# Four-layer linear-attention and MLP kernel: three chunks scaled in the second pass of layer 1, and the first MLP chunk's rows turned by VectorE and DMA

## The chip, the cores and the metric

The kernel runs on one core of a Trainium2 chip, in one launch. The metric is the device time of an execution in microseconds; times of several runs are given as their median. In the profile PE is TensorE's matrix product, PEld its weight load, DVE is VectorE, ACT is ScalarE, POOL is GpSimd and SP is SyncE, which issues all DMA transfers of this kernel.

## The reference

Four residual layers, A B A B, on x of 2048 tokens by 576 columns, with weights shared between the two A and the two B layers. A is linear attention with 32 heads of 18 columns; B normalizes once more and is an MLP with 4608 hidden columns.

```python
def _A_ref(x, wqkv, wo):
    B, S, D = x.shape
    H = 32; Dh = D // H
    qkv = (lambda x, *d: x.transpose(*d))((x @ wqkv).reshape(B, S, 3, H, Dh), 2, 0, 3, 1, 4)
    q, k, v = qkv[0], qkv[1], qkv[2]
    phi = lambda t: jnp.where(t > 0, t + 1, jnp.exp(t)) + 1e-6
    pq, pk = phi(q), phi(k)
    kv = jnp.einsum("bhsd,bhse->bhde", pk, v)
    z = jnp.einsum("bhsd->bhd", pk)
    num = jnp.einsum("bhqd,bhde->bhqe", pq, kv)
    den = jnp.einsum("bhqd,bhd->bhq", pq, z)[..., None] + 1e-6
    o = num / den
    return (lambda x, *d: x.transpose(*d))(o, 0, 2, 1, 3).reshape(B, S, D) @ wo

def _B_ref(x, w1, b1, w2, b2):
    y = _layernorm(x, axis=-1)
    h = _gelu(jnp.einsum("bsd,df->bsf", y, w1) + b1)
    return jnp.einsum("bsf,fd->bsd", h, w2) + b2

x = A_x
x = x + _A_ref(_layernorm(x, axis=-1), A_wqkv, A_wo)
x = x + _B_ref(_layernorm(x, axis=-1), B_w1, B_b1, B_w2, B_b2)
x = x + _A_ref(_layernorm(x, axis=-1), A_wqkv, A_wo)
x = x + _B_ref(_layernorm(x, axis=-1), B_w1, B_b1, B_w2, B_b2)
```

All inputs are bfloat16; the residual rows are kept in float32 in DRAM between the layers.

## The kernel before

The tokens are worked in 16 tiles of 128 rows and in 4 chunks of 512 (four tiles, `TPC`). The text calls the four layers 1 to 4; in the code `li` is 0 to 3. Normalized rows are needed with columns on partitions, as `yT` (5 blocks of 128 columns, the fifth only half filled with data). There are two ways to get them there, and the argument `evac` of `lnp.feed` chooses:

- `"act"` or `"dve"`: five TensorE transposes into PSUM (L493) and a copy to `yT`, by ScalarE at L498;
- `"dma"`: `turn_rows` lets VectorE transpose 32 by 32 blocks of a tile into the tile `turned` (L295); after the fourth tile of a chunk four DMAs store it to DRAM (`y_d`, L303), and `land` loads it back into `yT` (L320, L323) some ticks later. Tokens then stand in another order within the chunk, and `spread` and `gather` put that right where ScalarE reads PSUM.

`LNPipe` takes each tile through statistics, reciprocal deviation, the factors, the norm and the turn, one stage a `tick`. With statistics on VectorE these are L392, L393, L399 and L413; on ScalarE L374 and L383 with L385 on GpSimd. Then GpSimd does `ln_rstd` (L428), `ln_nmr` (L431), the norm of an MLP row (L461) and the copy of its last 64 columns to the upper half of the fifth block, the tail copy (L469). `hold` delays the first stage by so many ticks, `tp_at` sets after which output tile the TensorE transpose may stand.

Layer 1 (`layer_A` with `li == 0`) has a first pass over the keys of half the columns with most query products, and a second pass, `sums(n)`, which multiplies the other half of the keys with the rows. Into this second pass are woven: `den_stage(c)`, the denominators of a query chunk (20 small products, then Ln and Exp on ScalarE give `rden`); `quad_stage(c)`, which lays `rden` out for a product; `quarter_stage(c)`, 16 small products that broadcast `rden` into four PSUM banks, and four ScalarE copies (L792) of them into `turned`, which is free then; `scale_stage(4, c)`, the same for the last head group (L776); `quarter_scale(c, ...)`, which multiplies the queries with it on VectorE (L798); and `kv_groups` and `kv_wo_half` (L713, copied at L719), which fold the key-value matrix into the output weights. Before the change, chunks 0 and 1 go through these steps in the second pass, and 2 and 3 among the output tiles.

The output stage, `wo_stage(t)` for 16 tiles, has ten products a tile (L924) into one of two PSUM pairs by turns, `accA` and `accB`. VectorE adds the residual row (`residual`, L598), which frees the pair for the tile after next, and SP stores the new row. The first four tiles' rows feed the next MLP's first chunk, through `lnp.feed(..., "act", ...)`, that is TensorE transposes. Residual rows come in pairs of tiles (`prefetch_xo`), four tiles ahead.

PSUM has four banks by turns under the tag `h` (queries, denominators, broadcasts, folds, transposes and half of the MLP's first products) and the pairs `accA` and `accB`. The order of TensorE's instructions is the order of the code, held by `pe_chain`; on the other engines a scheduler places the instructions, within added orderings such as these:

```python
            if dve_last["sum"] is not None:
                tc.add_manual_dep(turn.ins, dve_last["sum"], NOSYNC, reason="rows are turned behind the sums")
```

The MLP (`LayerB`) takes one chunk after the other: nine groups of `m1_group` (L1053, gelu at L1049), then four tiles of 72 products (L1111). While a chunk is worked on, the next chunk's rows are loaded, normalized and turned through `"dma"`.

Of the kernel before, what the change touches and what calls it, by code (L numbers as in the profile page):

```python
# [8 lines left out]
ALU = mybir.AluOpType  # L9
# [25 lines left out]
def build(tc, A_x, A_wqkv, A_wo, B_w1, B_b1, B_w2, B_b2, out, dbg=None, n_layers=4):  # L35
    nc = tc.nc
    dbg = dbg or {}
    with ExitStack() as ctx:
# [90 lines left out]
        yT = const.tile([P, KD, S], BF16, name="yT")  # L129
# [162 lines left out]
        def turn_rows(y, t, kind):  # L292

            c, j = divmod(t, TPC)
            turn = nc.vector.transpose(out=turned[:, :, j, :], in_=y[:, 0:D])  # L295
# [15 lines left out]
        def land(now=False):  # L311

            for it in list(landing):
                it[0] -= 1
                if it[0] > 0 and not now:
# [3 lines left out]
                cols = slice(c * CB, (c + 1) * CB)  # L319
# [22 lines left out]
        class LNPipe:  # L342
# [11 lines left out]
            def tick(self, transposes=1):  # L354
                land()
                for it in list(self.items):
# [94 lines left out]
                    elif st in (2, 3):  # L451
# [16 lines left out]
                        if it["kind"] == "B" and it["evac"] != "dma":  # L468
                            nc.gpsimd.tensor_copy(out=y[:, D:DPAD], in_=y[:, 4 * P:D])  # L469
# [6 lines left out]
                    elif st == 4:  # L476
# [17 lines left out]
                        if first:  # L494
                            named(f"ca{t}", nc.scalar.copy(out=yT[:, 0:3, t * P:(t + 1) * P], in_=tp[:, 0:3, :]))  # L495
                            named(f"cd{t}", nc.vector.tensor_copy(out=yT[:, 3:KD, t * P:(t + 1) * P], in_=tp2[:, 3:KD, :]))
                        elif it["evac"] == "act":
                            turned_tile = nc.scalar.copy(out=yT[:, :, t * P:(t + 1) * P], in_=tp)  # L498
# [5 lines left out]
                        else:  # L504
                            nc.vector.tensor_copy(out=yT[:, :, t * P:(t + 1) * P], in_=tp)
# [102 lines left out]
        def layer_A(li, next_kind, pre_a1=None):  # L608
            pq = {}

            def q_proj(g, c, defer=False):
                qp = ps_h.tile([P, 512], F32, name="q_ps", tag="h")
                for k in range(KD):
                    pe(nc.tensor.matmul(qp[0:GR[g], :], lhsT=wqkv_sb[:, k, GO[g]:GO[g] + GR[g]],  # L614
                                     rhs=yT[:, k, c * CA:(c + 1) * CA],
# [26 lines left out]
            def k_half(t, half, defer=False):  # L642
                kp = ps_h.tile([P, 512], F32, name="k_ps", tag="h")
                for k in range(KD):
                    pe(nc.tensor.matmul(kp[:, 0:HALF], lhsT=yT[:, k, t * P:(t + 1) * P],  # L645
# [91 lines left out]
            def den_stage(c, after=None, pair=None):  # L737
# [10 lines left out]
                rden = work.tile([P, P], BF16, name="rden", bufs=1)  # L748
# [3 lines left out]
                act_last["rden"] = nc.scalar.activation(out=rden[:], in_=dp[:, P:2 * P], func=ACT.Exp,  # L752
# [4 lines left out]
            def quad_stage(c, after=None):  # L757
# [3 lines left out]
                    in1=rden_of.pop(c)[:].unsqueeze(1).to_broadcast([P, 4, P]), op=ALU.mult)  # L761
# [19 lines left out]
            def quarter_stage(c):  # L781
# [8 lines left out]
                spread_rows = turned[:].rearrange("p a t c -> p (a t c)").rearrange("p (i w) -> p i w", i=4)  # L790
# [3 lines left out]
            def quarter_scale(c, groups, after):  # L794
                spread_rows = turned[:].rearrange("p a t c -> p (a t c)").rearrange("p (i w) -> p i w", i=4)
# [54 lines left out]
            if li == 0:  # L850
# [369 lines left out]
```

## Time and profile before

| | |
|---|---|
| runs | 764.25, 763.88, 764.13 us; median 764.13 |
| profiled execution | 763.8 us, its span 762.1 us |
| granted TensorE clock | 1.0 |
| first product of the first MLP (h_ps) | 104.3 us after the span's start |
| layer 1, second pass; output stage | 59 to 81 us; 81 to 104 us |
| DMA | 80897 packets, 73.82 MB, 36730 of them under 512 B |

Times within the profile are microseconds from the span's start. Busy time of TensorE is a modelled end of each pipelined product, so the step from the start of one product to the start of the next is what a product costs: 0.123 for 288 columns, 0.216 for 512. A wait for several things is put down to the one that came last.

### The profile page before, as it was taken

The page shows a single profiled execution, that of the slowest core. Times are in us where ns is not written, and L with a number is a line of the kernel's source. Part 1 is how long each engine was busy: PE and PEld are TensorE (multiplying, and loading weights), DVE is VectorE, ACT ScalarE, POOL GpSimd, SP SyncE. Part 2 cuts the span into 40 slices and gives each one's busy share as a digit, 9 for nine tenths or more (in the row PEclk, how much of TensorE's full clock was granted, in tenths as well). Part 3 has the DMA queues.
Part 4 walks back from the last instruction along what each step waited for, and adds up shares of the span by engine and source line. Part 5 has one row for each costly group of instructions (what it writes and reads, how often), then busy time and mean ns, then how long its engine had stood idle before and what let it go on. Part 6 is the DMA issues. An engine that isn't in the chain of part 4 may idle for free.

```text
span 762.1 us, 15720 instructions
## 1 busy us (share of the span) xinstructions
PE 755.5 (99%) x6551; PEld 489.2 (64%) x6551; DVE 271.3 (36%) x684; ACT 328.7 (43%) x734; POOL 117.7 (15%) x194
## 2 busy tenths in 40 slices
PE   9999999999999999999999999999999999999998
PEld 5776764675477457646777767447645754674476
DVE  8875763136023503401355678600230132000000
ACT  6886657204600650264056567560164037205600
POOL 4840141002000301200110005300020021001000
PEclk9999999999999999999999999999999999999999
DMA  8993483017302711330246008430240033011000
GB/s 252 259 317 53 157 280 83 16 48 198 90 24 76 198 54 45 100 79 11 69 128 205 1 29 277 163 83 16 75 115 18 16 125 83 9 32 56 1 10 23
DMA packets 80897, 73.82 MB, mean 97 GB/s; under 512 B 36730, under 2 KB 65466, under 8 KB 80826
## 3 DMA queue, kind: packets, MB, share of 16 engines
q1 hardware_dynamic: 80826, 72.82, 32.3%
q8 instruction: 51, 0.84, 0.4%
q14 instruction: 20, 0.16, 0.1%
HBM read 48.03 MB, written 24.77 MB: 96 GB/s over the span
## 4 chain that ended last, share of the span: by engine, by line
PE 97%; DVE 1%; ACT 1%; DMA 0%; issue 0%
PE m_ps L1111 36%; PE h_ps L1053 20%; PE hp_ps L1053 16%; PE q_ps L614 6%; PE wo_ps L924 5%; PE k_ps L645 5%; PE k_ps L670 4%; PE m_half L1111 1%; PE k_tail L670 1%; PE tp L493 1%; PE kv_ps L695 0%; PE den_ps L745 0%; PE rden_ps L772 0%; PE rden_ps L788 0%; DMA x<-in_A_x_dram 0%; PE kvwo_half L713 0%
## 5 line engine op out<-in xcount | busy, mean ns | idle before, releaser
L1111 PE MATMUL m_ps<-w_sb,hT 128*128 128x288 bf16 x2232 | 274.8, 286 | 0.0
L1111 PEld LDWEIGHTS <-hT 128*128 128x128 bf16 x2304 | 224.8, 98 | 59.8 <-issue 3.4
L1053 PEld LDWEIGHTS <-w_sb 64*128 64x128 bf16 x2304 | 124.7, 94 | 136.4 <-issue 1.9
L1053 PE MATMUL hp_ps<-yT,w_sb 64*128 64x512 bf16 x1152 | 178.0, 376 | 0.0
L1053 PE MATMUL h_ps<-yT,w_sb 64*128 64x512 bf16 x1152 | 147.9, 376 | 0.0
L1058 ACT COPY relay_sb<-relay_sb 128x1 f32<-128x1 f32 x144 | 28.5, 198 | 259.9 <-PE h_ps L1053 217.6
L1049 ACT ACTIVATE hT<-h_ps,b1T 128x512 bf16<-128x512 f32 x144 | 91.0, 683 | 44.4 <-PE h_ps L1053 44.4
L428 POOL TENSOR_TENSOR ln_rstd<-ln_u,neg_half 128x1 f32<-128x1 f32 x61 | 35.3, 580 | 413.4 <-DVE ln_u L410 225.1
L1049 ACT ACTIVATE hT<-hp_ps,b1T 128x512 bf16<-128x512 f32 x144 | 91.1, 692 | 0.0
L598 DVE TENSOR_TENSOR xbf<-m_ps,xo 128x576 bf16<-128x576 f32 x15 | 11.4, 758 | 214.4 <-PE m_ps L1111 214.4
L598 DVE TENSOR_TENSOR xo<-m_ps,xo 128x576 f32<-128x576 f32 x16 | 12.1, 758 | 175.7 <-PE m_ps L1111 175.7
L581 POOL TENSOR_TENSOR xo<-xo,b_bc 128x576 f32<-128x576 f32 x32 | 40.9, 1282 | 98.8 <-DMA xo<-x_d 60.5
L1053 PE MATMUL h_ps<-yT,w_tail 64*128 64x512 bf16 x144 | 54.1, 376 | 0.0
L1053 PE MATMUL hp_ps<-yT,w_tail 64*128 64x512 bf16 x144 | 54.1, 376 | 0.0
L614 PE MATMUL q_ps<-yT,wqkv_sb 128*126 128x512 bf16 (+1 forms) x200 | 49.4, 379 | 0.0
L645 PE MATMUL k_ps<-wqkv_sb,yT 128*128 128x288 bf16 x320 | 47.1, 286 | 0.3 <-ACT yT L495 0.3
L924 PE MATMUL wo_ps<-kvwo,pq 126*128 126x288 bf16 (+1 forms) x320 | 43.7, 286 | 0.0
L1053 PEld LDWEIGHTS <-w_tail 64*128 64x128 bf16 x288 | 27.1, 94 | 17.0
L645 PEld LDWEIGHTS <-yT 128*128 128x128 bf16 x320 | 30.9, 98 | 8.9 <-ACT yT L495 1.1
L924 PEld LDWEIGHTS <-pq 126*128 126x128 bf16 (+1 forms) x320 | 30.0, 97 | 9.3 <-DVE pq L798 0.2
L614 PEld LDWEIGHTS <-wqkv_sb 128*126 128x126 bf16 (+1 forms) x200 | 25.6, 131 | 11.9 <-issue 0.3
L547 ACT ACTIVATE phi_e<-q_ps 126x512 bf16<-126x512 f32 (+1 forms) x40 | 23.9, 598 | 15.4 <-PE q_ps L614 15.4
(141 smaller groups left out, 597.9 us busy)
## 6 DMA issues: line engine op xcount, KB each, us to landing
xo<-x_d SPq DMA_DIRECT2D x48, 288.0 KB
x_d<-xo SPq DMA_DIRECT2D x32, 288.0 KB
xl<-x_d SPq DMA_DIRECT2D x24, 288.0 KB
y_d<-turned SPq DMA_DIRECT2D x40, 144.0 KB
w_sb<-in_B_w_dram SPq DMA_DIRECT2D x6, 864.0 KB
yT<-y_d SPq DMA_DIRECT2D x10, 512.0 KB
w_sb<-in_B_w_dram SPq DMA_DIRECT2D x9, 512.0 KB
x_d<-xn SPq DMA_DIRECT2D x16, 288.0 KB
```

Of the source, the lines that this page charges most:

```text
L428: nc.gpsimd.tensor_tensor(out=rstd[:], in0=it["u"][:], in1=neg_half[:], op=ALU.pow)
L547: exp = nc.scalar.activation(out=e_out, in_=ps_ap, func=ACT.Exp)
L581: nc.gpsimd.tensor_tensor(out=xo[:], in0=xo[:], in1=b2_bc[:], op=ALU.add)
L598: total = nc.vector.tensor_tensor(out=xn[:, cols].rearrange("p (h n) -> p h n", h=2), in0=halves, in1=xo[:, cols].rearrange("p (h n) -> p ...
L614: pe(nc.tensor.matmul(qp[0:GR[g], :], lhsT=wqkv_sb[:, k, GO[g]:GO[g] + GR[g]], rhs=yT[:, k, c * CA:(c + 1) * CA], start=(k == 0), stop=(k ...
L645: pe(nc.tensor.matmul(kp[:, 0:HALF], lhsT=yT[:, k, t * P:(t + 1) * P], rhs=wqkv_sb[:, k, D + half * HALF: D + (half + 1) * HALF], start=(k ...
L670: pe(nc.tensor.matmul(dst, lhsT=lhsT, rhs=pk, start=(t == 0), stop=(t == NT - 1)))
L924: pe(nc.tensor.matmul(wp[:, half, 0:HALF], lhsT=pq[(g, c)][0:GR[g], j * P:(j + 1) * P], rhs=kvwo[g][0:GR[g], half * HALF:(half + 1) * HALF ...
L1049: act_last["gelu"] = nc.scalar.activation(out=to, in_=ps, func=ACT.Gelu_apprx_tanh, bias=b1T[:, f:f + 1], scale=1.0).ins.name
L1053: mm = pe(nc.tensor.matmul(dst[n], lhsT=wt, rhs=mv, start=(seen[n] == 0), stop=(seen[n] == 8)))
L1058: relay = nc.scalar.copy(out=relay_sb[:, 1:2], in_=relay_sb[:, 0:1])
L1111: pe(nc.tensor.matmul(acc[half][:, 0:HALF], lhsT=hT[f][:, j * P:(j + 1) * P], rhs=w2_sb[:, f, half * HALF:(half + 1) * HALF], start=(f == ...
```

## The change

`yT` is laid out by row tile: a tile's five blocks stand side by side, and every product that reads a chunk reads four runs of 128 columns. `turned` and `y_d` are laid out to match: a partition's row of a chunk is 2560 elements in one piece, four stores write pieces of 640 elements, and one DMA (before two or three) loads a chunk back. For that the turned rows have 640 columns instead of 576, and the tail copy on GpSimd is made for every MLP row, also those that go through `"dma"`. `rden` moves from a tile of its own to a free corner of `turned`.

In layer 1, chunks 0, 1 and 2 go through denominators, broadcast and scaling in the second pass, and chunk 3 in the first output tiles. One fold half of groups 0 and 1 each moves to the other side of the pass; the products of groups 0 and 1 of the first two output tiles stand among the fold halves. The first MLP chunk of layer 2 gets its rows through `"dma"` instead of TensorE, with `hold` 3 for all four tiles, and its gelu writes in turned order like the other chunks. The first MLP chunk of layer 4 keeps TensorE's transposes. In all TensorE has 20 products fewer.

```diff
-        yT = const.tile([P, KD, S], BF16, name="yT")
+        yT = const.tile([P, NT, KD, P], BF16, name="yT")
-        turned = const.tile([P, D // 32, TPC, 32], BF16, name="turned")
+        turned = const.tile([P, 4, KD, TPC, 32], BF16, name="turned")
-        y_d = [dpool.tile([D // 32, 32, CB], BF16, name=f"y_d{i}") for i in range(2)]
+        y_d = [dpool.tile([P, TPC, DPAD], BF16, name=f"y_d{i}") for i in range(2)]
...
-            turn = nc.vector.transpose(out=turned[:, :, j, :], in_=y[:, 0:D])
+            turn = nc.vector.transpose(out=turned[:, :, :, j, :], in_=y[:].rearrange("p (k a c) -> p a k c", k=KD, a=4))
...
-                store = nc.sync.dma_start(out=home[:, :, i * P:(i + 1) * P].rearrange("j r n -> r j n"),
-                                          in_=turned[32 * i:32 * (i + 1), :, :, :].rearrange("r j t c -> r j (t c)"))
+                store = nc.sync.dma_start(out=home[:, i, :].rearrange("(a r) n -> r a n", a=4),
+                                          in_=turned[32 * i:32 * (i + 1), :, :, :, :].rearrange("r a k t c -> r a (k t c)"))
...
-                nc.sync.dma_start(out=yT[:, 0:KD - 1, cols],
-                                  in_=home[0:16, :, :].rearrange("(k jj) r n -> (jj r) k n", jj=4))
-                for hi in range(2 if kind == "B" else 1):
-                    landed = nc.sync.dma_start(out=yT[64 * hi:64 * (hi + 1), KD - 1, cols],
-                                      in_=home[16:18, :, :].rearrange("jj r n -> (jj r) n"))
+                landed = nc.sync.dma_start(out=yT[:, c * TPC:(c + 1) * TPC, :, :].rearrange("p b k n -> p b (k n)"), in_=home[:])
...
-                        if it["kind"] == "B" and it["evac"] != "dma":
+                        if it["kind"] == "B":
                             nc.gpsimd.tensor_copy(out=y[:, D:DPAD], in_=y[:, 4 * P:D])
...
-                                     rhs=yT[:, k, c * CA:(c + 1) * CA],
+                                     rhs=yT[:, c * TPC:(c + 1) * TPC, k, :],
...
-                rden = work.tile([P, P], BF16, name="rden", bufs=1)
+                rden = turned[:, 0, KD - 1, :, :].rearrange("p t c -> p (t c)")
...
-                den_stage(0)
-                quad_stage(0)
-                sums(2)
-                quarter_stage(0)
-                sums(1)
-                kv_groups((0, 1))
-                scale_stage(4, 0)
-                quarter_scale(0, (0, 1, 2, 3), after=dve_last["quad"])
-                q_proj(*q_left.pop(0))
-                sums(2)
-                den_stage(1)
-                quad_stage(1)
-                sums(2)
-                quarter_stage(1)
-                for half in range(4):
-                    kv_wo_half(half // 2, half % 2)
-                sums(1)
-                scale_stage(4, 1)
-                quarter_scale(1, (0, 1, 2, 3), after=dve_last["quad"])
-                sums(1)
-                q_proj(*q_left.pop(0))
-                sums(3)
+                for c in range(NCA - 1):
+                    den_stage(c)
+                    quad_stage(c)
+                    sums(2)
+                    quarter_stage(c)
+                    sums((1, 1, 2)[c])
+                    if c == 0:
+                        kv_groups((0, 1))
+                    if c > 0:
+                        kv_wo_half(c - 1, 0)
+                    if c < 2:
+                        sums(1)
+                    scale_stage(4, c)
+                    quarter_scale(c, (0, 1, 2, 3), after=dve_last["quad"])
+                    if c < 2:
+                        q_proj(*q_left.pop(0))
...
-                    lnp.feed(xn, t, "B", "pool", "act", hold=(2, 2, 6, 8)[t] if li > 0 else (2, 8, 8, 10)[t], tp_at=6 + 2 * t if li > 0 else (6, 10, 11, 14)[t],
-                             **(dict(after="sum") if t in (0, 3 if li > 0 else 2) else dict(stats="act", after="rden")))
+                    by_dve = t in (0, 3 if li > 0 else 2)
+                    lnp.feed(xn, t, "B", "pool", "act" if li > 0 else "dma", hold=(2, 2, 6, 8)[t] if li > 0 else 3,
+                             tp_at=6 + 2 * t, **(dict(after="sum") if by_dve else dict(stats="act", after="rden")))
...
                 q_proj(*q_left.pop(0))
+                kv_wo_half(0, 1)
+                kv_wo_half(1, 1)
                 kv_groups((2, 3, 4))
                 phi = q_proj(*q_left.pop(0), defer=True)
-                for half in range(2):
-                    for g in (2, 3, 4):
-                        kv_wo_half(g, half, by_dve=(g + half) % 2)
+                for g in (2, 3, 4):
+                    kv_wo_half(g, 0, by_dve=g % 2)
+                wo_products(0, (0, 1))
+                for g in (2, 3, 4):
+                    kv_wo_half(g, 1, by_dve=1 - g % 2)
+                wo_products(1, (0, 1))
                 phi(after=act_last["kvwo"])
...
                 wo_stage(t)
                 total = dve_last["sum"]
-                if c + 1 < NCA and not early:
+                if li == 0:
+
+                    if t == 0:
+                        den_stage(3)
+                        quad_stage(3, after=total)
+                    elif t == 1:
+                        quarter_stage(3)
+                        scale_stage(4, 3)
+                    elif t in (2, 3):
+                        quarter_scale(3, (2 * t - 4, 2 * t - 3), after=total)
+                elif c + 1 < NCA:
...
-                    to, ps = (hT[f][:, 0:CB], dst[n]) if c == 0 else (spread(hT[f][:, 0:CB]), gather(dst[n]))
+                    to, ps = (hT[f][:, 0:CB], dst[n]) if c == 0 and self.li > 1 else (spread(hT[f][:, 0:CB]), gather(dst[n]))
```

More of the change, by code (lines that the diff above doesn't have):

```diff
@@ L751, in den_stage @@
                     tc.add_manual_dep(log.ins, after, NOSYNC, reason="copies first")
-                act_last["rden"] = nc.scalar.activation(out=rden[:], in_=dp[:, P:2 * P], func=ACT.Exp,
+                act_last["rden"] = nc.scalar.activation(out=rden, in_=dp[:, P:2 * P], func=ACT.Exp,
                                                         scale=-1.0).ins.name
@@ L917, in kv_wo, with wo_products @@
                     act_last["kvwo"] = nc.scalar.copy(out=out, in_=wp[0:GR[g], :, 0:HALF]).ins.name
-            def wo_stage(t):
+            wo_open = {}
+            def wo_products(t, groups):
                 c, j = divmod(t, TPC)
-                wp = ps_acc.tile([P, 2, 512], F32, name="wo_ps", tag=("accA", "accB")[t % 2])
+                if t not in wo_open:
+                    wo_open[t] = 0, ps_acc.tile([P, 2, 512], F32, name="wo_ps", tag=("accA", "accB")[t % 2])
+                wp = wo_open[t][1]
+                wo_open[t] = groups[-1] + 1, wp
                 for half in range(2):
-                    for g in range(G):
+                    for g in groups:
                         pe(nc.tensor.matmul(wp[:, half, 0:HALF], lhsT=pq[(g, c)][0:GR[g], j * P:(j + 1) * P],
@@ L966, in layer_A @@
                     prefetch_xo(li, t + AHEAD + (li > 0), add_b2=False)
-                early = li == 0 and c == 0
                 if t == 0 and li > 0:
@@ L984, in layer_A @@
                         quad_stage(c + 2, after=total)
-                if t == 3:
+                if li > 0 and t == 3:
                     quad_stage(2, after=total)
@@ L1025, in half_blocks @@
                     rows = slice(64 * hi, 64 * hi + 64)
-                    ops = [(n, w1_sb[rows, k, f * P:(f + 1) * P], yT[rows, k, ctok]) for k in range(KD - 1)]
+                    ops = [(n, w1_sb[rows, k, f * P:(f + 1) * P], yT[rows, c * TPC:(c + 1) * TPC, k, :]) for k in range(KD - 1)]
                     if f % 2 == hi:
                         fc = f // 2 * P
-                        ops.append((n, w1_tail[rows, fc:fc + P], yT[rows, KD - 1, ctok]))
+                        ops.append((n, w1_tail[rows, fc:fc + P], yT[rows, c * TPC:(c + 1) * TPC, KD - 1, :]))
                     return ops
```

25 lines of the change are left out of this document (13 added, 12 removed).

## The prediction

> **What bounds the kernel now.** I read the page's busy shares and chain first, then TensorE's waits, then the timeline of each engine around the first attention layer's output stage (81 to 104 us), which the change rebuilds.
>
> ```profile
> PE 755.5 (99%) x6551; PEld 489.2 (64%) x6551; DVE 271.3 (36%) x684; ACT 328.7 (43%) x734; POOL 117.7 (15%) x194
> ...
> PE 97%; DVE 1%; ACT 1%; DMA 0%; issue 0%
> ```
>
> TensorE is the bound for the whole span, so a change is worth what it takes from TensorE's stream, less the waits it puts into it. The waits that the trace names are few (columns: us in total, times, longest):
>
> ```profile
> PE warm_ps L214 <- DVE y_ring L209: 1.3, 1, 1.3
> PE kvwo_half L713 <- ACT turned L792: 1.1, 3, 0.7
> PE k_ps L645 <- ACT yT L495: 0.3, 1, 0.3
> PE kvwo_half L713 <- ACT kvwo L719: 0.2, 1, 0.2
> ```
>
> All five transposes of a tile sit between two output products and cost their start-to-start step (TensorE's timeline: start, us, line, count):
>
> ```profile
> 94.75 2.63 PE L924 MATMUL wo_ps<-kvwo,pq 126*128 126x288 bf16 x20
> 97.22 0.44 PE L493 MATMUL tp<-ident,y_ring 128*128 128x128 bf16 x5
> 97.50 1.40 PE L924 MATMUL wo_ps<-kvwo,pq 126*128 126x288 bf16 x10
> ```
>
> Twenty products take 97.22 - 94.75 = 2.47 us, so one output tile is 1.235; the five transposes take 0.28. That stage is where VectorE is already busy 18.4 of 23.3 us (stretches by engine, columns as named in the answer):
>
> ```profile
> 81.00:104.30 23.30, 23.30 (x253) 17.29 (x251) 18.40 (x39) 14.13 (x31) 8.99 (x18) 1.00 0.70 237
> ```
>
> And this is how VectorE and GpSimd go about it:
>
> ```profile
> 87.20 0.85 DVE L759 TENSOR_TENSOR quad_rden<-quad_mask,rden 128x512 bf16<-128x512 bf16 x1
> ...
> 88.91 0.76 DVE L798 TENSOR_TENSOR pq<-pq,turned 126x512 bf16<-126x512 bf16 x2
> ...
> 91.59 0.75 DVE L598 TENSOR_TENSOR xn<-wo_ps,xo_pair 128x576 f32<-128x576 f32 x1
> 92.26 0.45 DVE L392 BATCH_NORM_STATS2 ln_st<-xn 128x6 f32<-128x288 f32 x1
> 92.63 0.44 DVE L393 BATCH_NORM_STATS2 ln_st<-xn 128x6 f32<-128x288 f32 x1
> ```
>
> ```profile
> 93.33 0.19 POOL L385 TENSOR_SCALAR ln_u<-ln_mv 128x1 f32<-128x1 f32 x1 [5.18 <-ACT ln_dump L383]
> 93.61 0.55 POOL L428 TENSOR_TENSOR ln_rstd<-ln_u,neg_half 128x1 f32<-128x1 f32 x1
> 94.26 0.26 POOL L431 TENSOR_SCALAR ln_nmr<-ln_mv,ln_rstd 128x1 f32<-128x1 f32 x1
> 94.62 0.82 POOL L461 TENSOR_SCALAR y_ring<-xn,ln_rstd,ln_nmr 128x576 bf16<-128x576 f32 x1
> ```
>
> ```profile
> 110.77 0.78 DVE L295 STREAM_TRANSPOSE turned<-y_ring 128x576 bf16<-128x576 bf16 x1
> ```
>
> Start to start, a residual sum holds VectorE 0.67 us, half the statistics 0.37, a scaling 0.34 (two in 0.68), a turn 0.71; for 640 columns instead of 576 I take 0.71 x 640/576 = 0.78. A tile's chain on GpSimd, from its rstd to the end of its tail copy (0.24 to 0.42), is about 2.2 us.
>
> **Part 1, transposes removed.** Four tiles of layer 1 lose five transposes each: 4 x 0.28 = -1.12 us on the path. ScalarE's four copies of 0.69 go too, off the path.
>
> **Part 2, the second pass.** The third chunk's denominators, broadcast and scaling move from the output stage into the pass of key sums. I followed the new order of TensorE's stream from 65.3 us (identical until then), adding the steps above, and let each instruction wait for what the built program makes it wait for. Of today's waits there, 0.23 (kv), 0.19 (q), 0.75 + 0.36 + 0.36 + 0.21 (the four kvwo halves, which ask for PSUM banks that ScalarE still copies, 0.48 a bank), 0.40 and 0.06, together 2.56, the change removes the kvwo burst. But chunks 1 and 2 now have the query product right ahead of their denominators: the exponential that gives the reciprocal is ready 1.7 us after the denominators' first product, TensorE after 1.45 (0.25 and 0.24); the bank rotation then costs 0.24 + 0.14, 0.11 + 0.27; the end of the pass 0.19 + 0.33 + 0.08 + 0.19; with kv's 0.23 that is 2.27. Net -0.3 us (bounds -2.6, all waits gone, and +1, if each of the three passes lost a bank's 0.36).
>
> **Part 3, the output stage.** Today TensorE loses 0.15 + 0.14 there, which vanish: -0.29. The new order puts the rest in its place. (a) The denominators of chunk 3 end on the last query group, whose VectorE pass ends about 83.9, while TensorE is there at 83.6: +0.4. (b) `scale_stage(4, 3)` follows `quarter_stage(3)` directly; its PSUM bank is the first one that ScalarE must copy out (0.46 after the broadcast starts, then 0.59): TensorE is there at 85.4, the copy ends at 86.05: +0.73. Today an output tile lies between. (c) The sum of tile 2 can start at 87.7. Behind it VectorE has, in this order, three scalings (1.0), sum 3 (0.67), two scalings (0.68), half the statistics (0.37), **the first turn** (0.78), the other half (0.37) and sum 4 (0.75): 0.67 + 1.0 + 0.67 + 0.68 + 0.37 + 0.78 + 0.37 + 0.75 = 5.3, to 93.0. Output tile 6 needs sum 4 (two PSUM buffers by turns) and TensorE is there at 91.4: +1.6, and 0.2 for tile 5 behind sum 3. (d) The second turn finds its rows ready, but turns 2 and 3 wait for GpSimd: tile 2's statistics end on VectorE near 93.9, and rstd, factor, norm, another tile's variance and the tail copy give 96.25, while VectorE was free at 95.4. Behind the waiting turn stands sum 7, for it output tile 9: turn 0.78, sum 0.75, so 97.85 against 96.75: +1.1. Turn 3 likewise (rows at 98.4), sum 8 and output tile 10: +0.9. Together 0.4 + 0.73 + 0.2 + 1.6 + 1.1 + 0.9 = 4.9.
>
> (e) The scalings of (c) run while GpSimd norms tile 0 (88.2 to 89.0). Trace: the quad above took 0.85 beside a norm, against 0.42 to 0.43 elsewhere, and a norm beside four scalings took 1.64 against 0.82. So VectorE loses 0 to 0.6 more there; I take 0.3. [...]
>
> **Part 4, landing.** Today's chunk 0 is in SBUF with ScalarE's last copy. Now turn 3 ends near 99.5; four stores follow on SP at about 0.45 each (the trace's 128-row issues take 0.32 to 0.45), then two row stores, then the load, which waits for the four stores. In today's trace four stores and their load need 4.9 us from the first store's issue to the load's (121.6 to 126.5) with 256 B pieces, and 512 KB more until 130; with 1280 and 5120 B pieces I take 3.5 and 3.5, so 106.5. Output tile 15 ends near 107.6, so the load costs nothing, with 1 us of cover. If it is later, TensorE waits for it directly. The last residual pair is issued behind the waiting load and lands about 107.5, just ahead of what needs it.
>
> **Part 5, at nothing.** Fewer and larger DMA pieces, one or two SP issues fewer per chunk, tail copies on GpSimd for each later MLP tile, turns longer by 0.08: all lie in MLP chunks where TensorE has 35 us stretches without a wait; if their cover went, a turn waiting on a tail copy (0.4) would be the price, once a tile. Gelu into turned order: 0.687 in chunk 0 and 0.684 in chunk 1, where it already is so. yT's new layout makes a product's 512 moving columns four runs of 128. No row has this; the nearest are 128-column transposes stepping 0.055 to 0.056 against 0.216 / 4 = 0.054, so 0 to 8 ns on a product; a gain is excluded, since no column is left out. I take 0.
>
> **Sum.** -1.12 - 0.3 - 0.29 + 4.9 + 0.3 = +3.5 us. The profiled execution took 763.8 (span 762.1 and 1.7 around it), 0.3 under the median of the runs, 764.13. 763.8 + 3.5 = 767.3; on the median 767.6. I say 767.5.
>
> **The rivals.** *Turns covered (faster side).* If rows are always ready before VectorE comes to their turn and VectorE has no backlog at sum 4, (c) to (e) vanish: -1.12 - 0.3 - 0.29 + 1.1 = -0.6 (763.5); with every wait of parts 2 and 3 gone too, -4.0 (760.1). It decides at the point where sum 4 would end by 91.4 and sum 7 by 96.7. For it: VectorE is idle for the second half of the stage (gaps of 0.3 to 0.8 before each sum from 98.9). Against: the order of its instructions is fixed, and 5.3 us of back-to-back work stand there. *Late landing.* The yT load sets the start of the MLP: each us behind 107.6 counts in full; DMA is 70% busy in this stage. Half a stage's queueing, 1 to 2.5 us, gives 768.6 to 770.1. *Slower reading.* At 4 to 8 ns on each of some 1500 steps of 512 columns, 6 to 12 us: 773 to 779. For it nothing, against it nothing but the transposes' step. *Partial.* GpSimd and VectorE each half a microsecond quicker at (c) and (d): +1.5 or less, 765.6.
>
> **Chances.** Forecast 0.62 (its own range 766 to 768.7), late landing 0.13, partial 0.13, turns covered 0.08, slower reading 0.04. About 0.2% (1.5 us) is what a measurement here can tell from no change: faster than 762.6 takes the better half of "covered", 0.05; within takes its rest and most of "partial", 0.13; slower 0.82. The range leaves out slower reading and the covered case, and takes in the rest: 764.8 to 770.1.
>
> **What the changed profile would show.** No L493 transposes on y_ring between 84 and 104 us. TensorE's idle before output products released by VectorE's sums, 1.6, 1.1 and 0.9 us ahead of tiles 6, 9 and 10, and 0.7 before the tail's broadcast. VectorE idle before two turns until GpSimd's tail copy. The first h_ps product near 107.8 instead of 104.33, and everything after it moved by that and no more. Wrong would be: that product before 105, idle there put down to the yT load, or h_ps products stepping other than 0.216 a pair.

## The result: 1.1% slower, and the profile after

Five executions of the changed kernel took 774.53, 772.13, 772.14, 770.56 and 773.32 us; the median is 772.14 against 764.1. The ratio worked out from all the runs is 1.0109, with the 95% interval 1.0097 to 1.0122 (the two medians alone give 1.0105). The prediction was 767.5, in a range that ended at 770.1: the sign was right, the size 4.6 us short. The five runs spread by 4 us where the kernel before spreads by 0.5, and they order themselves by the granted clock: 770.56 at 1.000, the three in the middle at 0.998, 774.53 at 0.996. The profiled execution is the slowest of them (774.53, span 772.8). Line numbers from here on are those of the kernel in question; in the changed one a sum is L593, an output product L918, a turn L295, the tail copy L464, the MLP's first products L1065.

The page of the changed kernel has 20 TensorE products fewer, as the change says, and a chain that is no longer TensorE alone:

```profile
PE 759.1 (98%) x6531; PEld 491.7 (64%) x6531; DVE 270.5 (35%) x688; ACT 326.3 (42%) x730; POOL 123.8 (16%) x218
...
PE 85%; DVE 1%; DMA 1%; POOL 1%; issue 0%; SPq 0%; ACT 0%; DVEq 0%
```

TensorE's waits (total us, times, longest) name the places:

```profile
PE wo_ps L918 <- DVE xn L593: 3.1, 3, 1.4
PE hp_ps L1065 <- DVE xn L593: 2.4, 1, 2.4
PE h_ps L1065 <- DMA yT<-y_d: 1.5, 1, 1.5
...
PE rden_ps L767 <- DVE xn L593: 0.6, 1, 0.6
```

The first is the output stage, foreseen at three tiles. The second and third are new, and TensorE's timeline (start, us, line, count, idle before) shows where they stand:

```profile
93.53 3.86 PE L918 MATMUL wo_ps<-kvwo,pq 126*128 126x288 bf16 x30 [1.43 <-DVE xn L593]
98.35 1.39 PE L918 MATMUL wo_ps<-kvwo,pq 126*128 126x288 bf16 x10 [0.97 <-DVE xn L593]
100.46 7.56 PE L918 MATMUL wo_ps<-kvwo,pq 126*128 126x288 bf16 x60 [0.71 <-DVE xn L593]
109.48 1.04 PE L1065 MATMUL h_ps<-yT,w_sb 64*128 64x512 bf16 x8 [1.46 <-DMA yT<-y_d]
110.34 0.38 PE L1065 MATMUL h_ps<-yT,w_tail 64*128 64x512 bf16 x1
113.11 1.89 PE L1065 MATMUL hp_ps<-yT,w_sb 64*128 64x512 bf16 x8 [2.40 <-DVE xn L593]
```

The output stage ends at 107.86, then the MLP waits for its rows until 109.48, works for one microsecond and waits again, this time for a residual sum. In the kernel before neither wait was there:

```profile
104.33 1.04 PE L1053 MATMUL h_ps<-yT,w_sb 64*128 64x512 bf16 x8
...
105.20 1.24 PE L1053 MATMUL hp_ps<-yT,w_sb 64*128 64x512 bf16 x8
```

Eight `hp_ps` products take 1.89 us instead of 1.24: the clock has fallen. The stretches by engine, with the granted clock as the third number from the end, say from when to when:

```profile
109.50:111.00 1.50, 1.21 (x9) 0.42 (x10) 0.00 (x0) 0.19 (x1) 0.00 (x0) 1.00 1.03 396
111.00:113.00 2.00, 0.00 (x0) 0.00 (x0) 0.70 (x2) 0.00 (x0) 0.00 (x0) 0.82 0.69 263
115.00:117.00 2.00, 2.00 (x12) 0.80 (x10) 0.00 (x0) 0.19 (x1) 0.00 (x0) 0.50 0.88 256
```

By the trace's clock records TensorE was granted half its clock from 112.27 on, for 6.83 us, and a pair of products stepped 0.427 instead of 0.216. SP's and VectorE's timelines tell why the sum came so late:

```profile
99.83 1.88 SPq L303 DMA_DIRECT2D y_d<-turned  x4
...
104.61 0.32 SPq L319 DMA_DIRECT2D yT<-y_d  x1
104.98 0.43 SPq L563 DMA_DIRECT2D xo_pair<-in_A_x_dram  x1
```

```profile
96.81 0.85 DVE L295 STREAM_TRANSPOSE turned<-y_ring 128x640 bf16<-128x640 bf16 x1 [1.04 <-POOL y_ring L464]
...
98.92 0.84 DVE L295 STREAM_TRANSPOSE turned<-y_ring 128x640 bf16<-128x640 bf16 x1 [0.62 <-POOL y_ring L464]
...
112.30 1.42 DVE L593 TENSOR_TENSOR xn<-wo_ps,xo_pair 128x576 f32<-128x576 f32 x2 [5.95 <-DMA xo_pair<-in_A_x_dram]
```

The yT load waits on SP until the four stores have landed, 104.6. The last residual pair (tiles 14 and 15) stands behind it, is issued at 104.98 and lands at 112.2; sum 14 runs only then, and it holds the PSUM pair `accA` that the first `hp_ps` products need.

The last product ends at 769.73 instead of 758.87, 10.86 later. M1 stands below for a chunk's first MLP products, from its first `h_ps` to its first `m_ps` product. In the order of time, each from starts of the same product in both traces: 0.28 is there before the second pass begins (the start-up; it lies between -0.1 and +0.5 in the other kernels' profiles below); 3.34 is the second pass and the output stage together; 1.53 the wait for the yT load; 2.75 the wait for the residual pair (3.63 from the first `h_ps` to the first `hp_ps` product, before 0.88); 2.95 the half clock (M1 of chunk 0 took 40.77 instead of 35.07, 5.70 more, of which 2.75 is that wait). From there on both traces run alike: chunk 1's M1 took 35.07 in both. This is the run that lost most to the clock: the median run is 1.6 us above the one at full clock (772.14 against 770.56).

### The profile page after: what moved, and what is told of

Read it like the earlier page. It is cut to its first block, busy times and chain, and to the rows that moved or that the text cites. A ratio compares the mean times of both kernels' runs of the same rounds, so it can differ in the third digit from the quotient of the medians.

```text
span 772.8 us, 15686 instructions
## 1 busy us (share of the span) xinstructions
PE 759.1 (98%) x6531; PEld 491.7 (64%) x6531; DVE 270.5 (35%) x688; ACT 326.3 (42%) x730; POOL 123.8 (16%) x218
## 4 chain that ended last, share of the span: by engine, by line
PE 85%; DVE 1%; DMA 1%; POOL 1%; issue 0%; SPq 0%; ACT 0%; DVEq 0%
PE m_ps L1123 35%; PE h_ps L1065 20%; PE hp_ps L1065 17%; PE q_ps L609 3%; PE wo_ps L918 3%; PE k_ps L640 3%; PE k_ps L665 2%; PE m_half L1123 1%; DMA xo_pair<-in_A_x_dram 1%; PE k_tail L665 1%; DVE xn L593 0%; DMA y_d<-turned 0%; DVE pq L793 0%; PE rden_ps L767 0%; DVE turned L295 0%
## 5 line engine op out<-in xcount | busy, mean ns | idle before, releaser
L1065 PEld LDWEIGHTS <-w_sb 64*128 64x128 bf16 x2304 | 126.3, 95 | 140.6 <-issue 9.3
L1065 PE MATMUL hp_ps<-yT,w_sb 64*128 64x512 bf16 x1152 | 176.2, 379 | 2.4 <-DVE xn L593 2.4
L1065 PE MATMUL h_ps<-yT,w_sb 64*128 64x512 bf16 x1152 | 152.7, 378 | 1.5 <-DMA yT<-y_d 1.5
L593 DVE TENSOR_TENSOR xbf<-m_ps,xo 128x576 bf16<-128x576 f32 x15 | 11.4, 757 | 214.1 <-PE m_ps L1123 214.1
L593 DVE TENSOR_TENSOR xo<-m_ps,xo 128x576 f32<-128x576 f32 x16 | 12.1, 758 | 176.0 <-PE m_ps L1123 176.0
L1065 PE MATMUL hp_ps<-yT,w_tail 64*128 64x512 bf16 x144 | 54.6, 380 | 0.0
L1065 PE MATMUL h_ps<-yT,w_tail 64*128 64x512 bf16 x144 | 54.4, 378 | 0.0
L918 PE MATMUL wo_ps<-kvwo,pq 126*128 126x288 bf16 (+1 forms) x320 | 43.0, 286 | 3.2 <-DVE xn L593 3.1
L295 DVE STREAM_TRANSPOSE turned<-y_ring 128x640 bf16<-128x640 bf16 x44 | 36.4, 833 | 11.2 <-POOL y_ring L464 11.1
L918 PEld LDWEIGHTS <-pq 126*128 126x128 bf16 (+1 forms) x320 | 30.4, 97 | 13.5 <-issue 4.4
L1065 PEld LDWEIGHTS <-w_tail 64*128 64x128 bf16 x288 | 27.2, 95 | 17.3 <-issue 0.5
```

The source lines that it names most:

```text
L295: turn = nc.vector.transpose(out=turned[:, :, :, j, :], in_=y[:].rearrange("p (k a c) -> p a k c", k=KD, a=4))
L593: total = nc.vector.tensor_tensor(out=xn[:, cols].rearrange("p (h n) -> p h n", h=2), in0=halves, in1=xo[:, cols].rearrange("p (h n) -> p ...
L918: pe(nc.tensor.matmul(wp[:, half, 0:HALF], lhsT=pq[(g, c)][0:GR[g], j * P:(j + 1) * P], rhs=kvwo[g][0:GR[g], half * HALF:(half + 1) * HALF ...
L1065: mm = pe(nc.tensor.matmul(dst[n], lhsT=wt, rhs=mv, start=(seen[n] == 0), stop=(seen[n] == 8)))
```

## The experiments

The theory after reading the two traces: the output stage costs what the prediction's sum says, about 3.5; the rest is the landing (the load, the pair behind it on SP) and a clock that falls because TensorE idles there. Rivals: the loss sits in the second pass or is larger in the output stage; the DMA is simply full, so that order on SP does not matter; the clock falls for a reason of its own. Each ratio below is against runs of the kernel before in the same series, whose medians lie between 763.85 and 764.19.

### The parts one by one: no_landing and tensore_turns

`no_landing` lets the first load land where the last chunk's rows will be, so that the first MLP chunk reads what already lies there, and issues the last pair one tile earlier, which puts it ahead of the load.

```diff
-landed = nc.sync.dma_start(out=yT[:, c * TPC:(c + 1) * TPC, :, :]...
+to = NCB - 1 if state["turns"] == 1 and c == 0 else c
+landed = nc.sync.dma_start(out=yT[:, to * TPC:(to + 1) * TPC, :, :]...
...
+                if li == 0 and t == 9:
+                    prefetch_xo(li, 14, add_b2=False)
...
```

> The changed kernel with the last residual pair ahead of the yT load, and the load of the first chunk's rows landing in the place of the last chunk's: the first MLP chunk then multiplies rows that lie there already, so nothing waits for the landing, while turns, stores and load are all still done. Theory 'the output stage costs the 3.5 us of the prediction and the landing the rest': the first h_ps product follows the output stage at once (107.4 to 107.9), clock 1.00, 767.6, range 767.0 to 768.3. Rival 'the landing hides a longer loss': 769 or more; rival 'the output stage costs little': under 766.

Measured: 766.99 (766.95 to 767.44), ratio 1.0037 (1.0024 to 1.0050), clock 1.00 in all five. M1 follows the output stage at once:

```profile
100.62 7.56 PE L919 MATMUL wo_ps<-kvwo,pq 126*128 126x288 bf16 x60 [0.71 <-DVE xn L594]
108.11 1.04 PE L1068 MATMUL h_ps<-yT,w_sb 64*128 64x512 bf16 x8
```

So turns, stores and the new second pass cost 2.9 us when nobody waits for the landing, near the 3.5 of the sum. The other 5.1 us of the median come from the two waits, for the load and for the pair, and the clock that falls with them.

`tensore_turns` keeps the layout and the second pass but gives the first chunk's rows back to TensorE's transposes and ScalarE's copies.

```diff
-lnp.feed(xn, t, "B", "pool", "act" if li > 0 else "dma", hold=(2, 2, 6, 8)[t] if li > 0 else 3,
-         tp_at=6 + 2 * t, ...
+lnp.feed(xn, t, "B", "pool", "act", hold=(2, 2, 6, 8)[t] if li > 0 else (2, 8, 8, 10)[t],
+         tp_at=6 + 2 * t if li > 0 else (6, 10, 11, 14)[t], ...
```

> The first MLP chunk's rows of layer 1 go through TensorE and ScalarE again, as before the change; the new yT layout and the three chunks scaled in the second pass stay. Theory 'the turns and their landing carry the loss': what is left is -0.14 (second pass) -0.29 (waits of before that vanish) +0.4 and +0.22 (denominators, reciprocal) +0.7 (broadcast behind the bank copies) +0.2 (sum 4 behind five scalings), so 764.1 + 1.1 = 765.2, range 764.5 to 766; clock 1.00 throughout; no wait ahead of tiles 9 and 10. Rival 'the second pass carries it': 768 or more.

Measured: 764.9, ratio 1.0013 (1.0004 to 1.0022), clock 1.00. The second pass and the later chunk cost 0.7 (764.19 in the same series); turning by VectorE and DMA costs the other 7.2, net of the 20 transposes that it saves.

### The clock: filled_wait and pair_fill

Products that nobody reads are put where TensorE waits.

```diff
+fill = ps_h.tile([P, 512], F32, name="fill_ps", tag="h") if li_fill(self.li, c, g) else None
+...
+        pe(nc.tensor.matmul(fill[:], lhsT=w1_sb[:, 0, 0:P], rhs=w1_sb[:, 0, 0:512], start=True, stop=True))
```

> The changed kernel, with products that nobody reads put where TensorE waits: 8 of 512 columns (1.7 us) ahead of the first h_ps product, 11 (2.4 us) ahead of the first hp_ps product. Theory 'TensorE's idle time of 4 us out of 5 brings the halved clock': clock 1.00 in all five runs, products step 0.216 a pair throughout, 769.5 to 771, spread under 1 us. Rival 'the clock falls whatever TensorE does there': clock 0.996 to 0.998 in most runs, 772 to 774.

Measured: 771.78, four runs within 0.12 us (771.70 to 771.82), clock 1.000 in each. With TensorE at work the clock did not fall in any of the four; without the filling it was 0.996 to 0.998 in four of the changed kernel's five runs. The time is above the expectation: filling of 1.7 and 2.4 us leaves no wait in front of `h_ps` and `hp_ps` in the trace, so part of it is probably itself delay.

`pair_first` has only the earlier pair; `pair_fill` has it and 12 filling products ahead of the first `h_ps` product.

> The last residual pair (rows of tiles 14 and 15) is issued ahead of the yT load instead of behind it; nothing else changes. Theory 'queue': the 2.4 us wait before the first hp_ps product is the pair standing in SP's queue behind the waiting load, so it falls to 0.5 or less; the yT load lands as before or up to 1 us later because it shares the DMA with 576 KB more, so the first h_ps product is at 109.5 to 110.5; with less idle time in a row the clock stays higher; 768.5 to 770.5. Rival 'transfer rate': the DMA engines are simply full, the wait moves from the pair to the yT load, the first h_ps product comes at 111 to 112, 771.5 to 773.

> The last residual pair ahead of the yT load, and 12 products of 512 columns (2.6 us) that nobody reads where TensorE waits for the load. Theory 'idle time halves the clock': clock 1.00 in all runs and a spread under 0.5 us, at 769.0 to 769.8 (the earlier version without the filling gave 769.38 in its one run at full clock). Against the filled version without the earlier pair (771.78) the pair's place is then worth 2 to 2.7 us. Rival 'one wait for the load is enough to drop the clock even when filled': 0.997, 771 to 774.

Measured: `pair_first` 772.39 (769.38 to 774.66), ratio 1.0108 (1.0090 to 1.0126); `pair_fill` 770.82 (770.25 to 770.94), clock 0.999 to 1.000. In stretches of 4 us, first of `pair_first`, then of `pair_fill`:

```profile
107.00:111.00 4.00, 1.32 (x12) 0.67 (x12) 1.02 (x2) 0.00 (x0) 0.00 (x0) 1.00 0.98 348
111.00:115.00 4.00, 4.00 (x24) 1.84 (x22) 0.00 (x0) 0.38 (x2) 0.00 (x0) 0.57 1.02 370
```

```profile
107.00:111.00 4.00, 3.36 (x20) 1.61 (x20) 1.08 (x2) 0.00 (x0) 0.00 (x0) 1.00 0.98 338
111.00:115.00 4.00, 4.00 (x38) 1.80 (x40) 0.00 (x0) 1.36 (x4) 0.00 (x0) 1.00 0.97 332
```

The DMA share was 0.98 in both, in the same stretch; after 1.32 us of work in four the clock was 0.57 in the next four, after 3.36 us it was 1.00. The wait ahead of `hp_ps` is gone in both, as the theory "queue" has it, but the time was missed: of the six runs only the one at full clock, 769.38, lies in the 768.5 to 770.5. The rival is half right: with the pair ahead of it the load took 5.6 us instead of 4.9 and the first `h_ps` product came at 110.38. The pair's place is worth 1.0 us (771.78 against 770.82), not 2 to 2.7, and in the unfilled median nothing that can be measured; nor did the clock stay higher there, at 0.996 to 1.000 as in the changed kernel.

### Is it SP, or the transfers? act_queue, stores_held

```diff
-store = nc.sync.dma_start(out=home...
+store = (nc.scalar if state["turns"] == 1 and i % 2 else nc.sync).dma_start(out=home...
-landed = nc.sync.dma_start(out=yT...
+landed = (nc.scalar if state["turns"] == 1 and c == 0 else nc.sync).dma_start(out=yT...
```

> The changed kernel with two of the first chunk's four stores and its yT load issued by ScalarE, which is idle there, the rest on SP. Theory 'SP's order': the stores are issued in 0.95 instead of 1.9 us, the residual pair no longer stands behind the waiting load and goes out near 102.5, so the 2.4 us wait ahead of hp_ps goes; the load is issued 0.5 us sooner, but shares the DMA with the pair, so the first h_ps product comes at 109 to 110; 769 to 770.5 plus what the clock does. Rival 'the transfer sets it': h_ps at 110.5 or later, 771 to 773.

Measured: 773.74 (773.18 to 774.96), ratio 1.0121 (1.0105 to 1.0136). The stores were all issued by 100.6 instead of 101.7 and yet the load could be issued only at 105.0. SP, free of the wait, sent the pair and the row stores right beside the load:

```profile
103.52 0.45 SPq L563 DMA_DIRECT2D xo_pair<-in_A_x_dram  x1
104.06 3.06 SPq L600 DMA_DIRECT2D x_d<-xn  x4
```

```profile
113.05 1.89 PE L1065 MATMUL h_ps<-yT,w_sb 64*128 64x512 bf16 x8 [5.15 <-DMA yT<-y_d]
```

The load took 8.0 us. The rival "the transfer sets it" stands, and the time is above even its 771 to 773. Issuing from two engines saved 1.1 us in starting the stores, and the load took 3.2 us longer (8.0 for 4.9).

`stores_held` is the opposite: pair ahead of the load, and the x_d stores of tiles 8 to 13 wait until it has landed.

```diff
+if li == 0 and 8 <= t < NT - 2:
+    held_rows.append((t, xn))
...
+    store = nc.sync.dma_start(out=x_d[late], in_=row)
+    tc.add_manual_dep(store.ins, state["landed"], SYNC, reason="rows are stored behind the landing")
```

> The changed kernel with the last residual pair ahead of the yT load, and the x_d stores of tiles 8 to 13 held until that load has landed. Theory 'shared DMA': the stores of turned rows and the load move 1.3 MB among 2.4 MB of other transfers; without the held 1.7 MB the four stores land 3 to 4 us after the first is issued instead of 4.8, the load takes 3 to 4 us instead of 4.8 to 5.6, the first h_ps product follows at 107.4 to 108.7, clock 1.00, 767 to 768.5. Rival 'fixed latency of two transfers in a row': h_ps at 109.5 or later, 769.5 to 772.

Measured: 767.76 (767.38 to 768.64), ratio 1.0051 (1.0037 to 1.0064); TensorE waits 0.3 us for the load.

```profile
99.60 1.88 SPq L303 DMA_DIRECT2D y_d<-turned  x4
101.52 0.71 SPq L565 DMA_DIRECT2D xo_pair<-in_A_x_dram  x1
104.01 0.34 SPq L319 DMA_DIRECT2D yT<-y_d  x1
107.98 1.30 SPq L607 DMA_DIRECT2D x_d<-xn  x3
```

From the first store's issue to the load's is 4.4 us and the load takes 4.1, against 4.8 and 4.9 in the changed kernel. Sharing the DMA cost 1.2 us of the 9.7; the 8.5 stay even so. The changed kernel's own trace says the same: its next chunk is stored and loaded in the middle of M1, with little beside it, and there the stores take 4.3 us (the kernel before, in the same place, 4.9):

```profile
131.46 1.87 SPq L303 DMA_DIRECT2D y_d<-turned  x4
135.80 0.34 SPq L319 DMA_DIRECT2D yT<-y_d  x1
```

The last packet of that load ended at 139.4; with the 0.5 us that passed for the first chunk from the load's last packet to the product (109.00 to 109.48), the two take an estimated 8.4 us. The two edits of `stores_held` give back 4.4 of the 8.0 us.

### The turns on VectorE: act_norms, turn_best, turn_mended

`act_norms` norms tiles 1 to 3 on ScalarE.

```diff
-lnp.feed(xn, t, "B", "pool", "act" if li > 0 else "dma", ...
+lnp.feed(xn, t, "B", "act" if li == 0 and t > 0 else "pool", "act" if li > 0 else "dma", ...
```

> The norms of tiles 1 to 3 (layer 1, first MLP chunk) on ScalarE instead of GpSimd, everything else as in the changed kernel. Theory 'turns 2 and 3 wait for GpSimd's chain': the rows are ready about 0.8 to 1.2 us sooner each, the waits of 1.1 and 0.9 us ahead of output tiles 9 and 10 fall under 0.4 each, turn 3 ends about 98 instead of 99.8, the yT load lands 1 to 1.5 us sooner, 769 to 770.5 (with what the clock does on top). Rival 'VectorE's own backlog': the waits stay at 0.7 or more, 772.

Measured: 771.91 (769.18 to 772.38), ratio 1.0091 (1.0078 to 1.0105); the runs at full clock are 769.2 and 769.9, against 770.6 for the changed kernel's. Ahead of output tile 10 the step beyond the usual one fell from 0.87 to 0.16, ahead of tile 9 only from 1.13 to 1.07: turn 2 still waited 1.04 for GpSimd's tail copy, because tile 2's statistics end on VectorE only behind the first turn and a sum. So the theory held for turn 3, the rival for turn 2, and the median lies at the rival's 772.

`turn_best` adds to `stores_held` these norms, ScalarE's statistics for tile 2, and the last chunk's tail broadcast behind output tile 2.

```diff
+by_dve = t in (0, 3) if li > 0 else t == 0
...
     elif t == 1:
         quarter_stage(3)
-        scale_stage(4, 3)
     elif t in (2, 3):
+        if t == 2:
+            scale_stage(4, 3)
```

> As the version before, and also: norms of tiles 1 to 3 on ScalarE, statistics of tile 2 on ScalarE instead of VectorE, the broadcast of the last chunk's tail behind output tile 2 instead of 1. Theory 'every loss of the output stage is a place in an engine's order': the waits of 0.7 (bank), 1.8 (sum 4), 1.1 and 0.9 (turns 2 and 3) fall to 0, 0.5 to 1.0, 0.3 and 0, the output stage ends near 105, turn 3 near 97, the load lands near 104.5; 764.2 to 766. Rival 'the turns themselves are too much for VectorE, or the landing decides again': 766.5 or more.

Measured: 773.24, ratio 1.0123 (1.0109 to 1.0137). The output stage ended at 106.1, a microsecond later than expected: the wait for the bank went and the one for sum 4 fell to 0.5, but output tile 7 now waited 1.5 us, where turn 1 waited 1.24 for GpSimd's tail copy. And the scheduler put the x_d stores of the last two tiles ahead of the load, and those wait for sums 14 and 15. SP's timeline and its waits:

```profile
105.85 1.57 SPq L609 DMA_DIRECT2D x_d<-xn  x2
107.61 0.32 SPq L319 DMA_DIRECT2D yT<-y_d  x1
```

```profile
SPq L609 <- DVE xn L595: 8.2, 4, 4.5
```

`turn_mended` puts those stores and the next chunk's row loads behind the load.

> The version before with its yT load no longer behind stores that wait for the last sums: all x_d stores from tile 8 on and the next chunk's row loads stand behind the load on SP. Theory 'SP's order made the 5.8 us wait': stores from 99.3, load issued 103.0 to 103.7, landed 106.5 to 107.5; the output stage ends near 106.1, so the wait is 0.4 to 1.4, clock 1.00 in most runs, the first h_ps product 2.3 to 3.2 us later than in the kernel before the change: 766.2 to 767.5. Rival 'the transfers take 9.6 us however little runs beside them': h_ps at 108.9 or later, 768.5 or more.

Measured: 767.69 (767.35 to 769.70), ratio 1.0058 (1.0044 to 1.0072). The load was issued at 103.86 and the first `h_ps` product came at 108.16: 8.8 us from first store to landing, later than expected, and the time is 0.2 above the expected range; two of the five runs had a clock of 0.997 and 0.998. The output stage ended 1.4 us earlier than in `stores_held` and none of it reached the end: turn 3 still ends at 99.3, because turns 1 and 3 wait 1.25 and 0.47 us for GpSimd's tail copies, and what follows it takes 8.5 to 8.8 us.

### A version that beats both? tt_later, tt_stats

From `tensore_turns`: the last chunk's stages one output tile later each; then also tile 2's statistics on ScalarE.

```diff
-if t == 0:
+if t == 1:
     den_stage(3)
...
-elif t in (2, 3):
-    quarter_scale(3, (2 * t - 4, 2 * t - 3), after=total)
+elif t in (3, 4):
+    if t == 3:
+        scale_stage(4, 3)
+    quarter_scale(3, (2 * t - 6, 2 * t - 5), after=total)
```

> The version that turns the first chunk's rows with TensorE, and the last chunk's denominators, broadcast and scaling one output tile later each (denominators behind tile 1, broadcasts behind tile 2 and 3, scalings behind 3 and 4). Theory 'each of these waits is a matter of place': the 0.4 (query pass), 0.2 (reciprocal) and 0.7 (bank copies) vanish, sum 4 or 5 waits 0.2 to 0.4 behind the scalings; 763.5 to 764.2 against 764.9 of the version before it and 764.19 of the kernel before the change. Rival 'the wait only moves to the sums': 764.6 or more.

> The version with TensorE's transposes and the later last chunk (764.3), with tile 2's statistics on ScalarE instead of VectorE. Theory 'VectorE's backlog of 0.5 us is what is left': 763.7 to 764.1, at most 0.05% under the kernel before the change. Rival 'no wait left to gain': 764.2 to 764.5.

Measured: `tt_later` 764.3, ratio 1.0002 (0.9993 to 1.0010), 0.6 below the version that it edits; `tt_stats` 764.11, ratio 1.0002 (0.9993 to 1.0011). The waits for denominators and bank copies were a matter of place, and one of 0.5 ahead of an output product was left (the line is of `tt_later`):

```profile
PE wo_ps L918 <- DVE xn L593: 0.5, 1, 0.5
```

In `tt_stats` it stands unchanged, so moving the statistics did not touch what that expectation named. Each is 0.2 us above the kernel before in its own series, and the two can't be told apart. Three chunks in the second pass then cost nothing, and gain nothing. No version run here beats the kernel before.

## Why the prediction was right up to the output stage and wrong behind it

**Part 1, transposes:** right; 20 products are gone, and with TensorE's transposes the count is 6551 again.

**Part 2, second pass:** forecast -0.3. Steps beyond the usual ones add up to 2.56 before, as the prediction lists them, and about 2.2 after, so about -0.35. (The -0.14 in the expectation of `tensore_turns` leaves out one step of 0.21.) The waits for the reciprocal are 0.24 and 0.24, named at 0.25 and 0.24.

**Part 3, output stage:** right nearly term by term. (a) 0.40 for 0.4, and 0.22 not foreseen: the quarter's products wait for the exponential as well. (b) 0.70 for 0.73; the profile names a sum as releaser, which ended at 86.58, but by the code the product takes a bank that ScalarE's copy must free, and the first copy ended at 86.54; moving the broadcast behind one more tile removed the wait (`turn_best`, `tt_later`). (c) 0.21 and 1.59 ahead of tiles 5 and 6 for 0.2 and 1.6. (d) 1.13 and 0.87 for 1.1 and 0.9. Together 5.1 for 4.9. (e) was taken at 0.3 on VectorE and is 0 there: GpSimd paid. Its norm beside the scalings took 1.77 instead of 0.83, while the three scalings from 88.91 to 89.98 kept 0.41 each:

```profile
88.92 1.77 POOL L456 TENSOR_SCALAR y_ring<-xn,ln_rstd,ln_nmr 128x576 bf16<-128x576 f32 x1
...
92.80 0.83 POOL L456 TENSOR_SCALAR y_ring<-xn,ln_rstd,ln_nmr 128x576 bf16<-128x576 f32 x1
```

The norm is longer by 0.94, and two of these scalings started after it (89.24 and 89.57) and were not slowed. In the kernel before, two scalings (97.20), not four, stood beside its norm of 1.64 (96.84), and they kept 0.41 as well; the norm beside the quad of 0.85 took 0.82 (86.96). So in that pair the quad was the longer one, in the other two the norm. The 0.3 was a choice between 0 and 0.6; the changed kernel's profile shows 0 on VectorE and 0.94 on GpSimd. The longer norm was hidden: VectorE did not wait for its rows before the first turn (91.66). The sum of parts 1 to 3 was 3.5; the traces give 3.34, and `no_landing`, built to show just this, 766.99 for 767.5. That the total fits so well is partly luck: the 0.22 that was not foreseen stands against the 0.3 of (e) that did not come.

**Part 4, landing:** this is the step that failed, in three places. First, the two transfers were mis-sized. "With 1280 and 5120 B pieces I take 3.5 and 3.5" had rows for 4.9 (from the first line to the second) and for 3.5, and shortened the first without one:

```profile
121.59 2.47 SPq L303 DMA_DIRECT2D y_d<-turned  x4
126.53 0.38 SPq L320 DMA_DIRECT2D yT<-y_d  x1
```

Measured were 4.8 and 4.9, together 9.7 for the 7.0 forecast, and 4.4 and 4.1 with less beside them. The larger pieces are worth 0.6 us (4.3 for 4.9 in the next chunk), not 1.4. Second, DMA was read as 70% busy, a mean of the whole stage. In the kernel before, the stretch in which the transfers were to run (last two numbers: DMA share, GB/s) was full:

```profile
99.50:104.30 4.80, 4.80 (x43) 3.68 (x40) 2.47 (x4) 1.21 (x2) 1.59 (x4) 1.00 0.99 347
```

Third, "the last residual pair is issued behind the waiting load and lands about 107.5, just ahead of what needs it" had the right mechanism and no price for a miss. It went out at 104.98 and took 7.2 us, and that wait cost more than the load's own, 2.75 against 1.53. Of the three the mean was the smallest miss: sharing the DMA accounts for the 1.2 us above.

**The rivals:** "late landing" was the case that came, at a chance of 0.13; its 768.6 to 770.1 priced the load alone. `pair_fill` and the one run of `pair_first` at full clock, 769.4 to 770.8, are about what it described. "Slower reading" is refuted: M1 of an undisturbed chunk takes 35.07 in both layouts. "Turns covered" is refuted by (c) and (d).

**Not in the prediction at all:** the clock. "Everything after it moved by that and no more" is false for M1 of chunk 0, which lost 2.95 us in the profiled run after TensorE had waited twice. Every microsecond of wait was counted as one; here about 4 us of wait cost 3 more in the profiled run; the median run lies 1.6 above the one at full clock.

**Part 5:** right. The turns took 0.80 to 0.85, and TensorE waits for none of them in a later chunk. VectorE's turns do wait for GpSimd's tail copies, 11.1 us over the whole kernel, but under cover.

## What to carry to other kernels

Work that moved from an engine to DMA traded a copy for two dependent transfers here, 9.7 us from the first store to the product that reads the rows, and 8.5 with less beside them (`stores_held`). Price their latency by a row of the same trace, read the DMA share in the very stretch in which they will run (0.99 here, where the stage's mean was 0.70), and list what stands behind the waiting load on its queue (here the pair, issued at 104.98). With the x_d stores moving beside them, another issuing engine or an earlier place passed the wait on from one transfer to the next: the pair was no longer waited for, but the load 5.1 us (`act_queue`) and 2.7 us (`pair_first`) instead of 1.5; with those stores held as well it was 0.3. When TensorE will wait, count the wait and the clock that it may lose (2.95 us here in the profiled run), and look at the spread of the runs: this kernel's lay between 770.56 at a clock of 1.000 and 774.53 at 0.996.

## What the runs showed of the hardware that was not expected

The granted clock fell in waits of a few microseconds. In the changed kernel the longest idle gap there was 2.4 us, in `pair_first` 2.7. From the end of the changed kernel's output stage to the fall (107.86 to 112.27) TensorE worked 1.40 us of 4.41; then the clock was 0.50 for 6.83 us, in which TensorE was busy for 5.99, and 1.00 again. In `pair_first` it was 0.57 over the four us from 111 and 1.00 over the next four.

The runs of one kernel differed in it, and more of them lost clock where TensorE waited longer. The waits are those ahead of the first `h_ps` and `hp_ps` products in the profiled run, the clock is the mean of each run:

| | waits, us | clock of the runs |
|---|---|---|
| `no_landing` | none | 1.000 in all five |
| `stores_held` | 0.3 | 1.000 in four, 0.997 in one |
| `turn_mended` | 1.8 | 1.000 in three, 0.997 and 0.998 |
| `act_norms` | 1.6 and 1.5 | 1.000 in two, 0.996 to 0.998 in three |
| changed kernel | 1.5 and 2.4 | 1.000 in one, 0.996 to 0.998 in four |
| `pair_first` | 2.7 | 1.000 in one, 0.996 to 0.998 in five |
| `act_queue` | 5.1 | 0.995 to 0.998 in all four |
| `turn_best` | 5.8 | 0.995 in all four |

What decides in which run of one kernel the clock falls, no run shows.

Four stores and the load behind them, 640 KB each way, took 8.5 us in `stores_held` and 13.4 in `act_queue`, by what else moved. In the changed kernel the same pass took 9.7 us, and 2.7 of it went by without a packet of theirs: 0.8 from the first issue to the first packet (99.83 to 100.65), 0.5 from the last stored packet to the load's issue (104.15 to 104.61), 1.0 to its first packet (105.58) and 0.5 from its last to the product (109.00 to 109.48). Packets moved in the other 6.9. Pieces of 1280 instead of 256 B hardly shortened the stores: 4.3 us in the next chunk against 4.9 in the kernel before.
